# Attention and gated MLP on one core: the first phase rearranged, and the copies of turned chunks written in program order

## The chip, the core and the metric

The kernel runs on one core of a Trainium2 chip. The core has a matrix engine (TensorE: PE in the profile, with PEld for its weight loads), a vector engine (VectorE, DVE), a scalar engine (ScalarE, ACT), a general engine (GpSimd, POOL), a sequencer that issues most transfers (SyncE, SP) and 16 DMA engines. On-chip memory is SBUF (128 partitions); matrix products land in eight PSUM banks of 128 x 512 floats. The metric is device microseconds of one execution.

## What is computed

```python
xn = _layernorm(x)                       # x: 2048 rows, D = 576
s = _A_ref(xn, wqkv, wo)                 # attention, 32 heads of 18, then times wo
g = _silu(_B_ref(xn, W_gate, W_up, W_down))   # relu(gate) * up, F = 4608, then W_down
return x + s * g
```

Attention is a full softmax over 2048 keys for each head. All of it is in float32.

## The kernel before

A float32 product is made of three fast ones. Each operand is split into a high and a low part (`hi`, `lo`), and `hi*hi`, `hi*lo` and `lo*hi` are summed in one PSUM bank. A split is a copy into the fast type (ACT or POOL), then a subtraction (DVE or POOL, `split_full` and `split_pool`).

**First phase.** The 2048 rows come in four groups of 512, g = 0 to 3. For a group, DVE takes mean and variance of the rows and normalizes them (`stats`, `normalize`, lines 345 to 380), ACT copies the last 64 columns of each row block a second time (line 379), PE turns the normalized rows (`turn`, tile `tps`), and the turned chunks are split into tiles `x` (`keep_x`, 5 tiles a group). Then come jobs: four of queries and keys (`qk_block`, bank `pq`, weights `wqk0` to `wqk3`, and `wqk4` for each second group), and four of values (`v_job`, bank `pv`, weights `wv` in three parts). A job has 30 products of a first part and 24 of a second. The second part of a job runs after the first part of the next one (`pending`, `flush`). The statistics and transposes of group g+1 are dealt into the jobs of group g, one step after each 7 pairs of products (`deal`). Group 0 is done by `first_rows`. `spill` writes the turned chunks of a group to DRAM (`xTd`), since SBUF does not hold all four. The raw weights `rgw` have two buffers, and POOL splits them in the order of the code.

**Second phase.** 144 units follow, 36 for each group of rows: unit k is a group and a block of 128 of the 4608 hidden columns. `up(k)` makes 27 steps for each of two row halves: nine chunks c of 64 features by three products. They are interleaved with products for the maxima of the scores (`pm`) and for the scores (`psx`). An odd unit ends with the products of probabilities and values (`attend`, `po`), an even one with the second MLP product of two units (`down`, `py`).

**Copies.** `load_x(g, c)` copies chunk c of group g from `xTd` into a tile of the pool `xA`, as two DMAs of 64 partitions by 1024 floats (256 KB each, below: a half). `xA` has 11 tiles and a group needs nine, so two are free while a group is in use. In the last unit of a group the next group's chunks 0 and 1 are asked for at the start, and chunk c+2 after the products of chunk c (lines 677 to 691):

```python
        if last:
            for c in range(2):
                load_x(units[k + 1][0], c)
...
                if t and last and n % len(PRODUCTS) == 2 and c + 2 < KC:
                    load_x(units[k + 1][0], c + 2)
```

`load_up(k)` fetches the raw `gate` and `up` weights of unit k (tile `rg` with a single buffer, units 3 to 15 in tiles `p`), `split_up(k)` splits them on POOL into `gw` (two buffers), and `load_down` and `split_down` do so for W_down (`rd`, `dw`).

**Order.** Products, DVE and POOL instructions stand in the order of the code. SP's are issued through `sp`, which pins that order while `sp.kept` is true. From unit 10 on it is false, and a scheduler may place SP's transfers ahead of others wherever a tile is free, unless one is pinned by itself. An engine works through its queue in order: an instruction that waits holds up those behind it.

Of the kernel before, what the change touches and what calls it, by code (L numbers as in the profile page):

```python
# [9 lines left out]
F32 = mybir.dt.float32  # L10
# [9 lines left out]
def kernel(  # L20
# [108 lines left out]

    def split_pool(hi, lo, raw, behind=None):  # L130
        cast = gp.tensor_copy(hi, raw)
        if behind is not None:
            after(cast, behind)
        gp.tensor_tensor(lo, raw, hi.bitcast(F32), ALU.subtract)
# [164 lines left out]
    def load_x(g, c):  # L299
        xc = xtile(xA)  # L300
        for t in range(2):
            sp.dma_start(
                xc[t * R : (t + 1) * R].rearrange("p a s -> p (a s)").bitcast(F32),
                xTd[g, c // 2, c % 2 * R : c % 2 * R + R],
            )
        xcur.setdefault(g, []).append(xc)

    with ExitStack() as st:
# [4 lines left out]

        def weights(name, n, parts, pl=one, held=None, behind=None, **kw):

            sl = WS if len(parts[0]) == 2 else XC
            gw = homes_w[name] if name in homes_w else pl.tile([P, 2, WS, n], F32R, name=name, **kw)
            gw = gw[:, :, :sl]
            o = 0
            for cols in parts:  # L320
                m = sum(c[2] for c in cols[0])
                rg = one.tile([P, WS, P], F32, name="rgw", bufs=2)[:, :sl, :m]
                load_nat(rg, cols)
                hi, lo = gw[:, 0, :, o : o + m], gw[:, 1, :, o : o + m]

                if held is not None:
                    held += [
                        lambda: pinned(nc.scalar.activation(hi, rg, AF.Copy)),
                        lambda: vec(nc.vector.tensor_tensor(lo, rg, hi.bitcast(F32), ALU.subtract)),
                    ]  # L330
                else:
                    split_pool(hi, lo, rg, behind)
                o += m
            return gw
# [35 lines left out]
        def normalize(xn, xt, js, mv, rs):  # L370

            for i, j in enumerate(js):
                pinned(
                    nc.vector.tensor_scalar(
                        xn[:, j, :D], xt[:, j], mv[:, i, 0:1], rs[:, i : i + 1],
                        op0=ALU.subtract, op1=ALU.mult,
                    )
                )
                pinned(nc.scalar.activation(xn[:, j, D:], xn[:, j, C4:D], AF.Copy))
                yield  # L380

        def new_xn():
            return one.tile([P, 4, XC * P], F32, name="xn")

        def turn(ps, xn, j, c):
            tp(ps[:, j * P : (j + 1) * P], xn[:, j, c * P : (c + 1) * P], ident)

        def keep_x(g, ps):
            xc = xtile(xA if g % 2 else xB)
            split_full(xc[:, 0], xc[:, 1], ps)  # L390
            xs[g].append(xc)

        def first_rows(xt, split_hi, split_lo):

            xn = new_xn()
            banks = [shared("tps") for _ in range(XC)]
            halves = [(0, 1), (2, 3)]
            a, b = (stats(xt, js) for js in halves)

            def finish(st_):  # L400
                try:
                    while True:
                        next(st_)
                except StopIteration as s:
                    return s.value

            def norm(js, ln):
                for _ in normalize(xn, xt, js, *ln):
                    pass

            for _ in range(3):
                next(a)
            next(b)
            ln = finish(a)
            for _ in range(2):
                next(b)
            norm(halves[0], ln)
            split_hi()
            norm(halves[1], finish(b))
            done = split_lo()  # L420
            for j in range(4):
                for c in range(XC):
                    turn(banks[c], xn, j, c)
            for ps in banks:
                keep_x(0, ps)
            return done

        def rows_to_features(g, xt):

            js = range(4)  # L430
            ln = yield from stats(xt, js)
            yield
            xn = new_xn()
            yield from normalize(xn, xt, js, *ln)
            yield
            for c in range(0, XC, 2):
                for d in range(c, min(c + 2, XC)):
                    ps = bank("tps")
# [4 lines left out]

        def spill(g):
            for c in range(XC):
                m = P if c < XC - 1 else R
                sp.dma_start(xTd[g, c, :m], xs[g][c][:m].rearrange("p a s -> p (a s)").bitcast(F32))

        njob = [0]

        def next_pair(name):
            njob[0] += 1
            if njob[0] % 3:
                return [shared(name) for _ in range(2)]
            return [shared(name), psO.tile([P, 512], F32, tag="po", name=name)]
# [13 lines left out]
        def flush():  # L469
            if pending:  # L470
                gens, done = pending.pop()
                run(*gens, P2)
                done()

        def job(outs, ops, done):

# [4 lines left out]
            for ins in fence:  # L481
                after(seen, ins)
            fence.append(seen)
            flush()
            pending.append((gens, done))
# [77 lines left out]
        qk_weights(0, held=held)  # L563
        w0_done = first_rows(rows0, *held)
        qk_weights(1, behind=w0_done)
        nxt = load_rows(1)
        qk_weights(2)
        qk_weights(3)
        wv = one.tile([P, 2, WS, HC], F32R, name="wv")

        def v_weights(m):
            rg = one.tile([P, WS, P], F32, name="rgw", bufs=2)[:, :, :VH]
            load_nat(rg, [[(wqkv, 2 * D + o * HC + m * VH, VH)] for o in range(2)])
            fs = slice(m * VH, (m + 1) * VH)
            split_pool(wv[:, 0, :, fs], wv[:, 1, :, fs], rg)

        for g in range(NQ):
            last = g == NQ - 1
            fill = rows_to_features(g + 1, nxt) if not last else None
            deal[:] = [fill, 7, 0]  # L580
            if last:
# [3 lines left out]
            for b in range(4):  # L585
# [22 lines left out]
                if b == 2 and last:  # L608
                    load_k(0, NQ - 1)
                if b == 1 and g == 0:  # L610
                    v_weights(0)
                    v_weights(1)
                if b == 2 and g == 0:
                    v_weights(2)
# [6 lines left out]
            if last:  # L621
# [9 lines left out]
                for j in range(4):  # L631
                    v_job(wv, g, j, homes[j]())
                    if j == 0:
                        split_up(1)
                deal[0] = None
                flush()
                for c in range(KC + 2 - XC, KC):
                    load_x(0, c)
            else:
                for j in range(4):  # L640
# [3 lines left out]
                    if j == 1:  # L644
                        spill(g)
                    if j and g == NQ - 2:
# [22 lines left out]
    def up(k):  # L669

        g, f = units[k]
        gw = gus.pop(k)
        if k % 2 and k < N1:
            ps = [psO.tile([P, 512], F32, name="po"), shared("pg2")]
# [195 lines left out]
    def emit_unit(k, ex, ns, mx, nm):  # L870
# [7 lines left out]
        split_up(k + 1)  # L878
        load_up(k + 2)
        if k == 10:  # L880
# [22 lines left out]
        for i, (l, r) in enumerate(zip(*order)):  # L903
            next(l)
            next(r)
            if i == 8 or (i == 30 and k % 2 == 0):
                gate_step()
        up_end(k, ps)
        run_tasks(tasks)
# [176 lines left out]
```

## Time and profile before

| | |
|---|---|
| median of 3 runs | 2606.31 us (2605.06 to 2606.45) |
| the profiled execution | 2609.54 us |
| its span | 2607.8 us |
| mean granted clock of TensorE | 0.998 |
| PE busy | 2585.0 us, 99% |
| DVE busy | 1907.1 us, 73% |

The profile is of one execution, so working in microseconds is set against 2609.54, of which 1.7 lie around the span. The page's slices show DMA at 0.7 of its time in the first tenth and at 0.2 to 0.5 in most of the rest.

### The profile page before, as it was taken

Reading aid. Unit: us, or ns where it says so; the run is one execution under the profiler, and the core shown is the slowest. Engines: PE = TensorE matmul, PEld = TensorE weight load, DVE = VectorE, ACT = ScalarE, POOL = GpSimd, SP = SyncE. Lnnn points to the kernel's source line nnn. Section 1 sums busy time; section 2 is a strip of 40 time slices with the busy share of each in tenths; the row PEclk is TensorE's granted clock in tenths of the full one; section 3 lists DMA queues with packets and bytes.
Section 4 is the critical chain, followed back from the end, with each engine's and each line's share of the span. In section 5 each row is a group of like instructions: output and inputs, shape, how many; then the busy total and the mean of one; then the engine's idle time right before and its main releaser. Section 6 shows DMA issues by size and latency. Waiting matters only on the chain.

```text
span 2607.8 us, 54045 instructions
## 1 busy us (share of the span) xinstructions
PE 2585.0 (99%) x21788; PEld 2040.1 (78%) x21788; DVE 1907.1 (73%) x3145; ACT 1383.4 (53%) x2594; POOL 1205.6 (46%) x971
## 2 busy tenths in 40 slices
PE   7999999999999999999999999999999999999999
PEld 6898887777777877777777777877777777777788
DVE  5435677888878888888877888888877888888145
ACT  2321135666565665555666556665556655556552
POOL 4245764444464444444455444444445444444554
PEclk9999999999999999999999999999999999999999
DMA  7777512333452322232363232322353322222245
GB/s 254 250 226 155 126 47 66 75 73 73 101 127 69 79 62 68 66 75 68 80 150 85 67 71 71 76 67 64 74 119 100 71 74 68 71 58 58 71 139 189
DMA packets 263802, 253.08 MB, mean 97 GB/s; under 512 B 27648, under 2 KB 208896, under 8 KB 263552
## 3 DMA queue, kind: packets, MB, share of 16 engines
q1 hardware_dynamic: 255808, 222.48, 34.7%
q0 software_dynamic: 7744, 27.14, 3.1%
q8 instruction: 172, 2.82, 0.5%
q14 instruction: 78, 0.64, 0.1%
HBM read 203.01 MB, written 46.01 MB: 95 GB/s over the span
## 4 chain that ended last, share of the span: by engine, by line
PE 96%; DMA 2%; POOL 1%; DVE 1%; issue 0%; ACT 0%; SPq 0%; POOLq 0%; DVEq 0%; ACTq 0%
PE pg L68 32%; PE py L68 18%; PE po L68 18%; PE pm L68 11%; PE psx L68 9%; PE pq L68 4%; PE pv L68 2%; PE pw L68 2%; DMA x<-xTd 1%; DMA rg<-in_B_W_up_dram 0%; PE tps L76 0%; POOL wv L85 0%; DMA rgw<-in_A_wqkv_dram 0%; DMA gx<-gd 0%; POOL gw L85 0%
## 5 line engine op out<-in xcount | busy, mean ns | idle before, releaser
L272 DVE TENSOR_REDUCE mx<-pm 128x1 f32<-128x512 f32 x2048 | 1365.0, 690 | 364.2 <-PE pm L68 208.3
L68 PE MATMUL pg<-x,gw 64*128 64x512 f32 x7560 | 1375.0, 394 | 4.4 <-POOL gw L85 3.5
L97 ACT ACTIVATE p<-psx 128x512 f32<-128x512 f32 x2048 | 1098.0, 603 | 478.1 <-PE psx L68 431.7
L68 PEld LDWEIGHTS pg<-x,gw 64*128 64x128 f32 x7560 | 1033.5, 187 | 94.7 <-issue 4.7
L85 POOL TENSOR_TENSOR hh<-h,hh 128x512 fp32r<-128x512 f32 x144 | 185.5, 1288 | 1007.8 <-ACT hh L97 970.8
L68 PEld LDWEIGHTS py<-dw,hh 128*128 128x128 f32 x3456 | 459.5, 188 | 25.6 <-DVE mx L272 17.4
L68 PE MATMUL py<-dw,hh 128*128 128x288 f32 x3456 | 476.4, 297 | 0.0
L68 PE MATMUL po<-p,va 128*32 128x512 f32 x4096 | 452.7, 594 | 0.0
L85 POOL TENSOR_TENSOR gw<-rg,gw 128x1152 fp32r<-128x1152 f32 x131 | 350.0, 2671 | 10.5
L68 PEld LDWEIGHTS po<-p,va 128*32 128x32 f32 x4096 | 126.5, 110 | 291.4 <-issue 280.8
L730 DVE TENSOR_TENSOR y<-py,y 128x288 f32<-128x288 f32 x544 | 236.8, 453 | 111.9 <-PE py L68 111.8
L68 PE MATMUL psx<-qT,kq 56*128 56x512 f32 x608 | 230.5, 392 | 0.0
L68 PE MATMUL pm<-kq,qT 54*128 54x512 f32 x608 | 228.2, 398 | 0.4 <-DVE mx L272 0.4
L85 POOL TENSOR_TENSOR dw<-rd,dw 128x576 fp32r<-128x576 f32 x144 | 206.5, 1434 | 11.5
L97 ACT ACTIVATE hh<-h 128x512 fp32r<-128x512 f32 x144 | 90.9, 631 | 214.3 <-DVE h L701 214.3
L68 PE MATMUL psx<-kq,kA 56*128 56x512 f32 x512 | 195.6, 393 | 0.2 <-DVE h L701 0.2
L68 PE MATMUL pm<-kq 54*128 54x512 f32 x512 | 195.3, 402 | 0.0
L68 PE MATMUL psx<-kq 56*128 56x512 f32 x512 | 194.8, 392 | 0.0
L68 PE MATMUL pm<-kA,kq 54*128 54x512 f32 x512 | 193.8, 400 | 0.2 <-DVE mx L272 0.2
L85 POOL CAST dw<-rd 128x576 fp32r<-128x576 f32 x144 | 95.9, 666 | 165.9 <-PE py L68 157.1
L68 PE MATMUL pm<-kA,qT 54*128 54x512 f32 x416 | 159.6, 402 | 0.0
L68 PE MATMUL psx<-qT,kA 56*128 56x512 f32 x416 | 157.6, 393 | 0.6 <-DVE gx L967 0.6
(92 smaller groups left out, 2251.6 us busy)
## 6 DMA issues: line engine op xcount, KB each, us to landing
rd<-in_B_W_down_dram SPq DMA_DIRECT2D x144, 288.0 KB
rg<-in_B_W_gate_dram SPq DMA_DIRECT2D x131, 288.0 KB
rg<-in_B_W_up_dram SPq DMA_DIRECT2D x131, 288.0 KB
x<-xTd SPq DMA_DIRECT2D x72, 256.0 KB
qd<-hh POOLq DMA_DIRECT2D x16, 512.0 KB, 5.2
kd<-hh POOLq DMA_DIRECT2D x16, 512.0 KB, 6.1
xTd<-x SPq DMA_DIRECT2D x16, 512.0 KB
kq<-kd SPq DMA_DIRECT2D x210, 36.0 KB
```

Source lines behind the costliest of these rows:

```text
L68: return tc.keep_in_program_order(nc.tensor.matmul(*args, **kw))
L85: return lambda *args, **kw: tc.keep_in_program_order(op(*args, **kw))
L97: i = op(*args, **kw)
L272: vec(nc.vector.tensor_reduce(mx[:, h, b, j, c : c + 1], ps, axis=AX.X, op=ALU.max))
L730: vec(nc.vector.tensor_tensor(ys[j][:, cs], ps, ys[j][:, cs], ALU.add))
```

## The change

The change has eight parts.

1. `load_x` is pinned: its DMAs stand on SP where the code has them.
2. `first_rows` makes one chain of statistics for four row blocks where there were two chains of two. 57 transposes of the identity into a bank of their own stand ahead. The high part of `wqk0` stands on ACT after the square root, and its low part is cut into four, two on DVE and two on POOL. The transposes go row block by row block.
3. The first job's two banks come from the pool `psG`, which the turned chunks do not use there.
4. The three raw parts of `wv` are loaded into tiles of `xA` early, and `wqk3` is split by ACT and DVE. POOL splits `wv` earlier. Group 1's steps are dealt after each 9 pairs.
5. The copies of the last columns (`twice`) are made together, ahead of chunk 2's transposes. Group 3's five tiles are taken together, and its fifth chunk gets the first of them, the one that comes free first.
6. The spill of group 0 is held until the first part of its second value job is through.
7. Unit 2's raw weights are loaded during the last value jobs and split at the end of unit 0. They were loaded at the start of unit 0.
8. The first 16 units take other PSUM banks: even ones and unit 15 the pair that odd ones had.

```diff
...
     def load_x(g, c):
         xc = xtile(xA)
         for t in range(2):
-            sp.dma_start(
-                xc[t * R : (t + 1) * R].rearrange("p a s -> p (a s)").bitcast(F32),
-                xTd[g, c // 2, c % 2 * R : c % 2 * R + R],
+            pinned(
+                nc.sync.dma_start(
+                    xc[t * R : (t + 1) * R].rearrange("p a s -> p (a s)").bitcast(F32),
+                    xTd[g, c // 2, c % 2 * R : c % 2 * R + R],
+                )
             )
         xcur.setdefault(g, []).append(xc)
 
...
                 hi, lo = gw[:, 0, :, o : o + m], gw[:, 1, :, o : o + m]
 
                 if held is not None:
-                    held += [
-                        lambda: pinned(nc.scalar.activation(hi, rg, AF.Copy)),
-                        lambda: vec(nc.vector.tensor_tensor(lo, rg, hi.bitcast(F32), ALU.subtract)),
-                    ]
+                    held += [hi, lo, rg]
                 else:
-                    split_pool(hi, lo, rg, behind)
+                    split_pool(hi, lo, rg)
                 o += m
             return gw
 
...
                         op0=ALU.subtract, op1=ALU.mult,
                     )
                 )
-                pinned(nc.scalar.activation(xn[:, j, D:], xn[:, j, C4:D], AF.Copy))
                 yield
+
+        def twice(xn, j):
+            pinned(nc.scalar.activation(xn[:, j, D:], xn[:, j, C4:D], AF.Copy))
 
         def new_xn():
             return one.tile([P, 4, XC * P], F32, name="xn")
 
+        homes_x = []
+
         def turn(ps, xn, j, c):
             tp(ps[:, j * P : (j + 1) * P], xn[:, j, c * P : (c + 1) * P], ident)
 
         def keep_x(g, ps):
-            xc = xtile(xA if g % 2 else xB)
+            xc = homes_x.pop(0) if g == NQ - 1 else xtile(xA if g % 2 else xB)
             split_full(xc[:, 0], xc[:, 1], ps)
             xs[g].append(xc)
 
-        def first_rows(xt, split_hi, split_lo):
+        def first_rows(xt, hi, lo, rg):
 
             xn = new_xn()
             banks = [shared("tps") for _ in range(XC)]
-            halves = [(0, 1), (2, 3)]
-            a, b = (stats(xt, js) for js in halves)
-
-            def finish(st_):
+            js = range(4)
+            steps = stats(xt, js)
+            while True:
                 try:
-                    while True:
-                        next(st_)
+                    next(steps)
                 except StopIteration as s:
-                    return s.value
-
-            def norm(js, ln):
-                for _ in normalize(xn, xt, js, *ln):
-                    pass
-
-            for _ in range(3):
-                next(a)
-            next(b)
-            ln = finish(a)
-            for _ in range(2):
-                next(b)
-            norm(halves[0], ln)
-            split_hi()
-            norm(halves[1], finish(b))
-            done = split_lo()
-            for j in range(4):
+                    ln = s.value
+                    break
+            pinned(nc.scalar.activation(hi, rg, AF.Copy))
+            for j, _ in enumerate(normalize(xn, xt, js, *ln)):
+                twice(xn, j)
                 for c in range(XC):
                     turn(banks[c], xn, j, c)
+            rest = []
+            for s0 in (0, XC):
+                for on, ss in ((nc.vector, slice(s0, s0 + 2)), (None, slice(s0 + 2, min(s0 + XC, WS)))):
+                    args = lo[:, ss], rg[:, ss], hi[:, ss].bitcast(F32), ALU.subtract
+                    if on is None:
+                        rest.append(args)
+                    else:
+                        done = vec(on.tensor_tensor(*args))
+            for args in rest:
+                after(gp.tensor_tensor(*args), done)
             for ps in banks:
                 keep_x(0, ps)
-            return done
 
         def rows_to_features(g, xt):
 
             js = range(4)
             ln = yield from stats(xt, js)
             yield
+            if g == NQ - 1:
+                homes_x[:] = [xtile(xA) for _ in range(XC)]
+                homes_x.append(homes_x.pop(0))
             xn = new_xn()
             yield from normalize(xn, xt, js, *ln)
             yield
             for c in range(0, XC, 2):
+                if c == 2:
+                    for j in js:
+                        twice(xn, j)
                 for d in range(c, min(c + 2, XC)):
                     ps = bank("tps")
                     for j in js:
...
                     keep_x(g, ps)
                 yield
 
-        def spill(g):
+        def spill(g, behind=None):
             for c in range(XC):
                 m = P if c < XC - 1 else R
-                sp.dma_start(xTd[g, c, :m], xs[g][c][:m].rearrange("p a s -> p (a s)").bitcast(F32))
+                out_ = sp.dma_start(xTd[g, c, :m], xs[g][c][:m].rearrange("p a s -> p (a s)").bitcast(F32))
+                if behind is not None:
+                    after(out_, behind)
 
         njob = [0]
 
         def next_pair(name):
             njob[0] += 1
+            if njob[0] == 1:
+                return [bank(name) for _ in range(2)]
             if njob[0] % 3:
                 return [shared(name) for _ in range(2)]
             return [shared(name), psO.tile([P, 512], F32, tag="po", name=name)]
...
                 run(*gens, P2)
                 done()
 
+        marks = []
+
         def job(outs, ops, done):
 
             fence = []
...
             for ins in fence:
                 after(seen, ins)
             fence.append(seen)
+            marks.append(seen)
             flush()
             pending.append((gens, done))
 
...
 
         held = []
         qk_weights(0, held=held)
-        w0_done = first_rows(rows0, *held)
-        qk_weights(1, behind=w0_done)
+        warm = bank("warm")
+        for _ in range(57):
+            tp(warm[:, :P], ident, ident)
+        first_rows(rows0, *held)
+        qk_weights(1)
         nxt = load_rows(1)
+        wvs = []
+
+        def load_v(m):
+            rg = xtile(xA).bitcast(F32).rearrange("p a s -> p (a s)")[:, : WS * VH]
+            rg = rg.rearrange("p (c f) -> p c f", f=VH)
+            load_nat(rg, [[(wqkv, 2 * D + o * HC + m * VH, VH)] for o in range(2)])
+            wvs.append(rg)
+
+        load_v(0)
         qk_weights(2)
-        qk_weights(3)
+        held = []
+        qk_weights(3, held=held)
+        load_v(1)
+        load_v(2)
         wv = one.tile([P, 2, WS, HC], F32R, name="wv")
 
         def v_weights(m):
-            rg = one.tile([P, WS, P], F32, name="rgw", bufs=2)[:, :, :VH]
-            load_nat(rg, [[(wqkv, 2 * D + o * HC + m * VH, VH)] for o in range(2)])
             fs = slice(m * VH, (m + 1) * VH)
-            split_pool(wv[:, 0, :, fs], wv[:, 1, :, fs], rg)
+            split_pool(wv[:, 0, :, fs], wv[:, 1, :, fs], wvs[m])
 
         for g in range(NQ):
             last = g == NQ - 1
             fill = rows_to_features(g + 1, nxt) if not last else None
-            deal[:] = [fill, 7, 0]
+            deal[:] = [fill, 7 if g else 9, 0]
             if last:
                 spill(g)
             if g % 2:
...
                     load_up(1)
                 if b == 2 and last:
                     load_k(0, NQ - 1)
+                if b == 0 and g == 0:
+                    v_weights(0)
                 if b == 1 and g == 0:
-                    v_weights(0)
+                    hi, lo, rg = held
+                    pinned(nc.scalar.activation(hi, rg, AF.Copy))
+                    vec(nc.vector.tensor_tensor(lo, rg, hi.bitcast(F32), ALU.subtract))
                     v_weights(1)
-                if b == 2 and g == 0:
                     v_weights(2)
                 if b == 1 and g == 1:
                     nxt = load_rows(g + 2)
...
                     v_job(wv, g, j, homes[j]())
                     if j == 0:
                         split_up(1)
+                    if j == 2:
+                        load_up(2)
                 deal[0] = None
                 flush()
                 for c in range(KC + 2 - XC, KC):
...
                     if j == 0 and g == 0:
                         nxt = load_rows(g + 2)
                     if j == 1:
-                        spill(g)
+                        spill(g, marks[-1] if g == 0 else None)
                     if j and g == NQ - 2:
                         for c in range(2 * j - 2, 2 * j):
                             load_x(0, c)
...
 
         g, f = units[k]
         gw = gus.pop(k)
-        if k % 2 and k < N1:
+        if k < N1 and (k % 2 == 0 or k == N1 - 1):
             ps = [psO.tile([P, 512], F32, name="po"), shared("pg2")]
         else:
             ps = [bank("pg0"), bank("pg1")]
...
         if k not in rds and k not in dws:
             load_down(k)
         split_up(k + 1)
-        load_up(k + 2)
+        if k:
+            load_up(k + 2)
         if k == 10:
             sp.kept = False
         run_later()
...
             next(r)
             if i == 8 or (i == 30 and k % 2 == 0):
                 gate_step()
+        if k == 0:
+            split_up(2)
         up_end(k, ps)
         run_tasks(tasks)
         if k % 2:
```

On SP at the first group change (units 34 to 37), these rows stand before; `x<-xTd` is a half, `rg` the raw weights of a unit, `rd` those of W_down, and `qT<-nr` writes row maxima:

```order
L97 DMA rd<-in_B_W_down_dram 128x576
L97 DMA x<-xTd 64x1024
L97 DMA rg<-in_B_W_gate_dram 64x9x128
L97 DMA rg<-in_B_W_up_dram 64x9x128
L97 DMA x<-xTd 64x1024 x13
L97 DMA rd<-in_B_W_down_dram 128x576
L97 DMA rg<-in_B_W_gate_dram 64x9x128
L97 DMA rg<-in_B_W_up_dram 64x9x128
L97 DMA qT<-nr 2x8x32 x8
L97 DMA kq<-qd 18x1024 x3
L97 DMA kA<-kd 18x512 x6
L97 DMA kq<-qd 18x1024 x3
```

After the change the same place of SP reads:

```order
L97 DMA rd<-in_B_W_down_dram 128x576
L97 DMA rg<-in_B_W_gate_dram 64x9x128
L97 DMA rg<-in_B_W_up_dram 64x9x128
L301 DMA x<-xTd 64x1024 x18
L97 DMA rd<-in_B_W_down_dram 128x576
L97 DMA rg<-in_B_W_gate_dram 64x9x128
L97 DMA rg<-in_B_W_up_dram 64x9x128
L97 DMA qT<-nr 2x8x32 x8
L97 DMA kA<-kd 18x512 x6
L97 DMA kq<-qd 18x1024 x2
```

Before, one half stands ahead of the two `rg` transfers and 13 behind; the first four of the 18 stand far ahead, near unit 0 (below). After it all 18 stand in one row behind `rg`. The order moves alike at the other two group changes, where four of the 18 stood right behind the change before.

On POOL at the start, from the identity to the first two jobs' stores (`qd`, `kd`), before:

```order
masks.py:199 AFFINE_SELECT ident<-ident 128x128
L85 CAST wqk_209<-rgw 128x1152
L85 TENSOR_TENSOR wqk_209<-rgw,wqk_209 128x1152
L85 CAST wqk_219<-rgw 128x1152
L85 TENSOR_TENSOR wqk_219<-rgw,wqk_219 128x1152
L85 CAST wqk_109<-rgw 128x1152
L85 TENSOR_TENSOR wqk_109<-rgw,wqk_109 128x1152
L85 DMA qd<-hh 128x2x512
L85 DMA kd<-hh 128x2x512
L85 CAST wv<-rgw 128x9x96
L85 TENSOR_TENSOR wv<-rgw,wv 128x9x96
```

and after:

```order
masks.py:199 AFFINE_SELECT ident<-ident 128x128
L85 TENSOR_TENSOR wqk_110<-rgw,wqk_110 128x384
L85 TENSOR_TENSOR wqk_110<-rgw,wqk_110 128x256
L85 CAST wqk_255<-rgw 128x1152
L85 TENSOR_TENSOR wqk_255<-rgw,wqk_255 128x1152
L85 CAST wqk_270<-rgw 128x1152
L85 TENSOR_TENSOR wqk_270<-rgw,wqk_270 128x1152
L85 CAST wv<-x 128x9x96
L85 TENSOR_TENSOR wv<-x,wv 128x9x96
L85 DMA qd<-hh 128x2x512
L85 DMA kd<-hh 128x2x512
```

`wqk1` now stands behind two pieces of `wqk0`'s low part, `wqk3` is gone from POOL, and the first part of `wv` stands ahead of the first store.

On SP around units 0 to 2, before:

```order
L97 DMA kq<-kd 18x512 x6
L97 DMA qT<-qd 18x1024 x12
L97 DMA kA<-kd 18x512 x6
L97 DMA x<-xTd 64x1024 x8
L97 DMA rd<-in_B_W_down_dram 128x576
L97 DMA rg<-in_B_W_gate_dram 64x9x128
L97 DMA rg<-in_B_W_up_dram 64x9x128
L97 DMA x<-xTd 64x1024 x2
L97 DMA rd<-in_B_W_down_dram 128x576
L97 DMA p<-in_B_W_gate_dram 64x9x128
L97 DMA p<-in_B_W_up_dram 64x9x128
```

and after:

```order
L97 DMA kq<-kd 18x512 x6
L97 DMA qT<-qd 18x1024 x12
L97 DMA rg<-in_B_W_gate_dram 64x9x128
L97 DMA rg<-in_B_W_up_dram 64x9x128
L97 DMA kA<-kd 18x512 x6
L301 DMA x<-xTd 64x1024 x6
L97 DMA rd<-in_B_W_down_dram 128x576
L97 DMA rg<-in_B_W_gate_dram 64x9x128
L97 DMA rd<-in_B_W_down_dram 128x576
L97 DMA p<-in_B_W_gate_dram 64x9x128
L97 DMA p<-in_B_W_up_dram 64x9x128
```

Unit 2's `rg` has moved from behind eight halves to the place ahead of `kA` and of six halves; the four halves of the next group (two of the eight, and the two behind `rg`) have gone from here.

## Rows read from the trace of the kernel before

**Rows 1.** The page's part 1: busy time, share and instructions by engine.

```profile
PE 2585.0 (99%) x21788; PEld 2040.1 (78%) x21788; DVE 1907.1 (73%) x3145; ACT 1383.4 (53%) x2594; POOL 1205.6 (46%) x971
```

**Rows 2.** Timeline from the start: start, us, engine, line, operation [idle before <-releaser].

```profile
9.61 3.68 PE L76 MATMUL tps<-ident,xn 128*128 128x128 f32 x20 [9.61 <-DVE xn L374]
...
10.85 1.07 DVE L374 TENSOR_SCALAR xn<-xt,mv,ln 128x576 f32<-128x576 f32 x2
...
12.89 2.56 ACT L127 ACTIVATE x<-tps 128x512 fp32r<-128x512 f32 x5 [0.68 <-PE tps L76]
...
14.26 18.43 PE L68 MATMUL pq<-x,wqk 64*128 64x512 f32 x154 [0.97 <-DVE x L128]
...
14.49 2.68 POOL L85 TENSOR_TENSOR wqk<-rgw,wqk 128x1152 fp32r<-128x1152 f32 x1
```

**Rows 3.** Chain that ended last, first phase: start us, us, what.

```profile
35.36 4.86 DMA rgw<-in_A_wqkv_dram
...
43.33 3.37 PE pv L68 x26
...
156.25 24.95 PE pq L68 x214
```

**Rows 4.** Timeline of DVE, POOL and PE, 7 to 61 us.

```profile
7.44 0.17 DVE L366 TENSOR_SCALAR ln<-ln 128x2 f32<-128x2 f32 x1
...
23.58 2.54 DVE L366 TENSOR_SCALAR ln<-ln 128x4 f32<-128x4 f32 x1
...
31.57 2.15 POOL L85 TENSOR_TENSOR wv<-rgw,wv 128x864 fp32r<-128x864 f32 x1
...
32.63 1.09 PE L76 MATMUL tps<-ident,xn 128*128 128x128 f32 x8
...
49.30 10.94 PE L68 MATMUL pv<-wv,x 64*128 64x288 f32 x162
```

**Rows 5.** Stretches of PE alone: us, PE busy (x), PEclk, DMA share, GB/s.

```profile
9.60:12.30 2.70, 2.69 (x13) 1.00 1.00 351
...
10.00:20.00 10.00, 8.92 (x65) 1.00 0.64 194
...
40.00:50.00 10.00, 7.51 (x70) 0.83 0.88 277
```

**Rows 6.** Chain that ended last, units 0 to 4.

```profile
206.50 11.11 DMA rg<-in_B_W_up_dram
...
230.97 6.54 PE py L68 x48
...
251.74 6.57 PE py L68 x48
```

**Rows 7.** Timeline of PE, units 0 and 2.

```profile
202.91 1.63 PE L68 MATMUL pg<-x,gw 64*128 64x512 f32 x10 [0.47 <-ACT ev L532]
...
221.66 2.08 PE L68 MATMUL pg<-x,gw 64*128 64x512 f32 x8 [1.97 <-POOL gw L85]
```

**Rows 8.** Timeline of SP at the first group change.

```profile
695.29 0.48 SPq L97 DMA_DIRECT2D x<-xTd  x1
...
698.74 0.61 SPq L97 DMA_DIRECT2D rg<-in_B_W_gate_dram  x1
...
700.07 10.48 SPq L97 DMA_DIRECT2D x<-xTd  x13
```

**Rows 9.** Three group changes: us, PE, PEld, DVE, ACT, POOL busy, PEclk, DMA, GB/s.

```profile
703.00:718.00 15.00, 15.00 (x134) 8.51 (x133) 9.52 (x17) 8.56 (x16) 6.17 (x7) 1.00 1.04 231
...
1318.00:1332.00 14.00, 14.00 (x128) 8.12 (x122) 8.47 (x15) 7.60 (x15) 5.43 (x5) 1.00 1.04 235
...
1931.00:1945.00 14.00, 14.00 (x126) 7.77 (x124) 8.50 (x16) 7.66 (x15) 6.17 (x7) 1.00 1.04 242
```

**Rows 10.** Timeline of PE, last chunk at the first and second change.

```profile
719.95 0.74 PE L68 MATMUL pg<-x,gw 64*128 64x512 f32 x4 [0.40 <-DMA x<-xTd]
...
1333.55 0.86 PE L68 MATMUL pg<-x,gw 64*128 64x512 f32 x5
```

More of the change, by code (lines that the diff above doesn't have):

```diff
@@ L128, in split_full, with split_pool @@
         nc.vector.tensor_tensor(dlo, ps, dhi.bitcast(F32), ALU.subtract)
[L130 to L133, printed above, removed]
+    def split_pool(hi, lo, raw):
+        gp.tensor_copy(hi, raw)
         gp.tensor_tensor(lo, raw, hi.bitcast(F32), ALU.subtract)
@@ L312, with weights @@
         hx = pool(xBs, "hx", 4, "right")
-        def weights(name, n, parts, pl=one, held=None, behind=None, **kw):
+        def weights(name, n, parts, pl=one, held=None, **kw):
             sl = WS if len(parts[0]) == 2 else XC
```

## The prediction

> **What bounds the kernel now.** First the busy times: PE works 2585.0 of 2607.8 us [rows 1]. So only two kinds of time can be won: PE waiting, some 23 us in all, and PE at half clock. A loss is anything that makes PE wait anew. I read the chain that ended last for where something other than PE stands in it, then the timelines there. Four places come out.
>
> *The start.* The first transpose waits for the first normalized rows until 9.61 [rows 2]. Twenty of them take 3.68 us, where later eight take 1.09 [rows 4]: the first 13 take 2.69 [rows 5], 0.207 each against 0.136, which I read as half clock, though that row's clock column has 1.00. A backlog of them stands before the last rows' five. The last normalization ends at 11.92 (10.85 + 1.07), the first split begins at 12.89, and the first product at 14.26 [rows 2].
>
> *Group 0's value weights.* From 14.26 to 49.30 PE does 216 `pq` products at 0.1166 (24.95 / 214, [rows 3]), 20 transposes at 0.136 (1.09 / 8) and 30 `pv` products at 0.0675 (10.94 / 162, [rows 4]): 25.2 + 2.7 + 2.0 = 29.9 us. The stretch is 35.04, so 5.1 are lost. They lie at the `pv` products: the chain goes through the load of raw weights at 35.36 and resumes on PE at 43.33 [rows 3], and the ten microseconds from 40 hold 7.51 busy at a mean clock of 0.83 [rows 5].
>
> *Units 0 to 2.* Unit 2's weights are asked for at 206.50 and land 11.11 us later [rows 6], and PE waits for their split up to 221.66 [rows 7]. Two units and one `py` group take 251.74 - 230.97 = 20.77 us, 14.23 of it the two units [rows 6]. Three units should take 21.35; from 202.91 to 230.97 they took 28.06. So 6.7 are lost here, half clock included.
>
> *The group changes.* At the first, SP issues one half of the copies at 695.29, then the weights from 698.74, then 13 halves from 700.07 on [rows 8]. From 703 to 718 the DMA engines are busy all the time (1.04) and move 231 GB/s; at the other two changes it is 235 and 242 [rows 9]. A half is 262 144 bytes, so it takes 1.135, 1.116 and 1.083 us. PE is busy throughout, but only just: the last chunk's products wait for a copy at the first change, and at the second they start at 1333.55 with no wait noted [rows 10].
>
> **The change part by part.** *Start (parts 2, 3).* One chain of statistics in place of two saves seven small DVE steps at 0.17 [rows 4], 1.2; the wait for ACT's root, which the other chain's statistics covered, comes back, and I take 0.7 for it: 0.5 earlier. The 57 transposes begin with the identity, near 1.3, when PE has nothing else. If 13 of them run at 0.207 as the old ones did [rows 5] and 44 at 0.136, they end at 10.0, about when the first rows are normalized (some 9.9), so they cost nothing; all 57 at 0.207 would end at 13.1 and push the real ones back by 3.2. At full clock twenty take 2.7 instead of 3.68; of these 0.96, 0.65 are on the path, since ACT's tail copy stands between the last normalization and the first split. The first product comes 1.15 earlier, at 13.1. Own banks save the second bank's wait for one more split, an ACT step of 2.56 / 5 = 0.51 [rows 2]: 0.5, bounds 0 and 0.6. Against this, POOL begins `wqk1` only after two pieces of `wqk0`. By size, 384 and 256 of 1152 columns at 2.68 [rows 2] are 1.5 us, from about 12.0, when DVE's pieces end; copy and subtraction of `wqk1`, 3.8 with the 2.68, then end near 17.5 with the steps between. The second job, at 13.1 + 30 x 0.1166 = 16.6, asks for the low part in its third pair, near 17.0. The cost is 0.5 to 0.9, take 0.7; bounds 0 and 1.5. Start: 1.15 + 0.5 - 0.7 = **0.95 gained**.
>
> *Value weights (part 4).* With their own tiles the raw parts land without waiting for `rgw`, and POOL splits them earlier. A part's subtraction is 2.15 on POOL [rows 4], and its copy goes before it. I count 4.6 of the 5.1 as winnable, leaving 0.5 for bank waits. What takes it back: group 1's steps are dealt after 9 pairs, and their small DVE steps now meet a POOL queue without gaps. Row L366 takes 0.17 alone and 2.54 while POOL subtracts [rows 4], 2.4 more. One such hit before the transposes, 2.0 with what is slack, and 0.3 for banks: -2.3, with bounds 0 and -4.6. Rest: **2.3 gained**.
>
> *Spill, tail copies, tiles (parts 5, 6), banks (8).* The held spill goes out a few us later, and what it writes is read back only in the second phase; behind it SP has loads for later groups, covered by group 0's jobs. The tail copies stand on ACT, 53% busy [rows 1], and are wanted by the last chunk only. The fifth chunk's tile comes earlier. Taking other banks ends the wait of unit 0 for an evacuation: 0.47 [rows 7], **0.5 gained**; the even units' banks are evacuated under the products that follow.
>
> *Unit 2's weights (part 7).* They stand ahead of six halves and are split at the end of unit 0, ahead of `hh(0)` on POOL, which is delayed by a split (3.8), but is used only behind unit 2. The wait and the half clock go: **6.7 gained**. Next late would be chunk 8 of group 0, behind the weights by 576 KB; four halves have left this place, so I cost it at nothing (bound: one half, 1.1).
>
> *Copies (part 1).* All 18 halves stand on SP behind the weights that go out at 698.74, where five stood ahead [rows 8]. At a DMA that is full already, five more halves shift the last landing by 5 x 1.135 = 5.7, 5 x 1.116 = 5.6 and 5 x 1.083 = 5.4. I take 0.5 off the second, where no wait is noted [rows 10]: 5.7 + 5.1 + 5.4 = 16.2 lost. Nothing covers it: the products of the first unit read the chunks in order and have no other work beyond `pm` and `psx`. PE then works in pieces, and the clock may fall. From 40 to 50, with 7.51 us busy, it averaged 0.83, which cost 1.7 us; from 10 to 20, with 8.92 busy, it was 1.00 [rows 5]. A unit of some 10 us stretched to 15 lies below both, but its waits are of one half each, about 1.1, like the 0.97 ahead of the first product [rows 2] that cost no clock. I take 1.0 for the three changes, bounds 0 and 5.1 (three times 1.7). **17.2 lost.**
>
> The Trainium skill speaks of the rate: "DMA: Bandwidth & Descriptors", section Bandwidth, has 341 GB/s for one transfer of 1 MB. By it five halves would be an estimated 3.84 us and the sum some 5 us lower. The trace shows 231 to 242 at full engines, and the measurement decides.
>
> *Sum.* 0.95 + 2.3 + 0.5 + 6.7 = 10.45 gained, 17.2 lost: +6.75 on 2609.54, or 2616.3 in its profile's terms. On the median, 2606.31 + 6.75 = **2613.1 us**. Its own range, from the bounds: downwards 3.5 if the early gain is whole, 1.0 if the clock holds and 1.2 for one half of slack, 5.7; upwards 4.1 for the clock, 3.25 if start and values gain nothing, and 1.1 for chunk 8, 8.4: 2607.4 to 2621.5.
>
> **The rivals.** *A. The early gain is whole.* POOL and DVE do not collide, `wqk1` is in time, all 5.1 of the value weights come back: 1.65 + 5.1 + 0.5 + 6.7 = 13.95; the clock holds at the changes, 16.2 lost: +2.3, 2608.6. For it: DVE's slow step needs POOL at work in that very moment. Against: POOL's queue has no gap now.
>
> *B. The copies go faster.* The ten microseconds from 40 show 277 GB/s at a share of 0.88, 315 at a full one [rows 5]. At that rate five halves are 4.2 us: 12.5 + 1.0 lost, less 10.45: +3.0, 2609.3. Against it: the same 64-partition copies ran at 231 to 242 at all three changes [rows 9].
>
> *C. The copies are hidden anyway.* The halves start ahead of the weights after all, or the first unit of a group tolerates them: nothing lost, 2606.31 - 10.45 = 2595.9. Against it: the wait at 719.95 [rows 10] and SP's order.
>
> *D. The first phase gains nothing.* The steps of group 1, dealt later and held by POOL, come late to the values; PE waits for them and the clock falls, as from 40 to 50 [rows 5]. That takes all of the first two gains once DVE's chain loses over 3.3 us to POOL, less than two hits of 2.4 [rows 4]: 7.2 gained, 17.2 lost: +10.0, 2616.3. With the copies as in C this would still be faster; so the sign hangs on the copies.
>
> **How the numbers follow.** A change of 0.2%, 5.2 us, is about what a measurement can tell from none: faster is below 2601.1, slower above 2611.5. Forecast 0.50, A 0.17, B 0.10, C 0.11, D 0.12. C gives faster: 0.11. Slower are D and nearly all of the forecast's own range above 2611.5, with a little of A and B: 0.12 + 0.42 + 0.06 = 0.60. Same: 0.29. The range of 2604 to 2621.5 leaves out C and the ends where D meets a falling clock, together under 0.2.
>
> **What would show it.** On SP one row of 18 halves at each change, behind the weights. On PE, waits for `x<-xTd` that sum to about 5 us in the first unit of groups 1, 2 and 3, where now there is one of 0.40. No wait for `gw` in unit 2, none for `wv` at 41 to 43, the first transposes at full clock, and the first product near 13.1. If PE does not wait at the changes, or by less than 3 us each, step "copies" is wrong, and with it the sign. If unit 2 still waits, or group 0's values do, the gains are.

## The result and the profile after

The changed kernel takes 2619.73 us (median of 6 runs, 2616.8 to 2620.61), the kernel before 2606.34 beside it: a ratio of 1.005, 95% interval 1.0037 to 1.0063. It is 13.4 us slower, where 6.8 were forecast. Sign and place were right, both sizes were off: the group changes cost 1 to 3 us more than forecast, and the early gain was some 4 us less.

The page of the changed kernel, part 1:

```profile
PE 2595.6 (99%) x21845; PEld 2039.3 (78%) x21845; DVE 1907.2 (73%) x3141; ACT 1385.3 (53%) x2594; POOL 1204.6 (46%) x971
```

PE has 57 products more, the ones at the start, and they take 7.95 of the 10.6 us by which it is longer "busy" than in [rows 1]. Half-clock stretches count as work too, but both profiles have 10.2 us of them. The span is 2617.5 us.

**The group changes.** The timeline of SP at the first one, after:

```profile
685.96 0.36 SPq L97 DMA_DIRECT2D rd<-in_B_W_down_dram  x1
689.83 0.60 SPq L97 DMA_DIRECT2D rg<-in_B_W_gate_dram  x1
690.49 1.48 SPq L97 DMA_DIRECT2D rg<-in_B_W_up_dram  x1
692.02 14.99 SPq L301 DMA_DIRECT2D x<-xTd  x18
```

This is [rows 8] with all 18 halves behind the weights. SP stands still for 3.5 us ahead of the weights, and the 18 halves stand still with it. The raw weights `rg` have a single buffer, and POOL was still splitting what lay in it:

```profile
687.12 2.69 POOL L85 TENSOR_TENSOR gw<-rg,gw 128x1152 fp32r<-128x1152 f32 x1
```

The split ends at 689.81 and the weights go out at 689.83; it is the same to 0.03 us at the other two changes and in the kernel before. The timeline of PE in the first unit of groups 1, 2 and 3, its waits alone:

```profile
706.59 0.49 PE L68 MATMUL pg<-x,gw 64*128 64x512 f32 x1 [0.44 <-DMA x<-xTd]
708.62 0.50 PE L68 MATMUL pg<-x,gw 64*128 64x512 f32 x1 [0.59 <-DMA x<-xTd]
710.67 0.49 PE L68 MATMUL pg<-x,gw 64*128 64x512 f32 x1 [0.50 <-DMA x<-xTd]
713.57 0.50 PE L68 MATMUL pg<-x,gw 64*128 64x512 f32 x1 [1.68 <-DMA x<-xTd]
...
1334.16 0.50 PE L68 MATMUL pg<-x,gw 64*128 64x512 f32 x1 [0.83 <-DMA x<-xTd]
1336.42 0.96 PE L68 MATMUL pg<-x,gw 64*128 64x512 f32 x5 [0.82 <-DMA x<-xTd]
...
1953.57 0.79 PE L68 MATMUL pg<-x,gw 64*128 64x512 f32 x1 [1.54 <-DMA x<-xTd]
```

[Rows 10] had one wait of 0.40 at the first change and none at the second. The idle shown is only what lies between modelled ends of products; the whole is read from the starts. From its first product to the one after its last, the unit takes 16.58, 15.13 and 16.79 us at the three changes, and took 11.16, 10.28 and 10.57 in the first profile of the kernel before; after the first change the next products (`py`) take 1.58 more, at half clock. Together 18.1 us.

The windows of the changed kernel there (us, PE, PEld, DVE, ACT, POOL busy, PEclk, DMA share, GB/s):

```profile
692.00:707.00 15.00, 14.56 (x127) 7.91 (x126) 9.38 (x16) 7.88 (x15) 6.17 (x7) 1.00 1.01 252
707.00:722.00 15.00, 12.20 (x67) 8.85 (x64) 7.40 (x12) 6.01 (x10) 1.27 (x1) 0.77 0.74 170
1314.00:1329.00 15.00, 14.50 (x127) 7.83 (x125) 8.79 (x15) 7.66 (x15) 5.44 (x5) 1.00 1.06 252
...
1934.00:1949.00 15.00, 13.58 (x115) 6.61 (x109) 8.31 (x15) 7.10 (x13) 6.17 (x7) 1.00 1.05 244
1949.00:1964.00 15.00, 12.89 (x85) 10.61 (x81) 8.17 (x15) 4.82 (x8) 1.37 (x2) 0.89 0.73 150
```

The DMA engines are as full as in [rows 9] while the halves land. The clock falls behind the waits at the first and the third change: 0.77 and 0.89 of 15 us is 3.4 and 1.7 us worth of clock. At the second, with waits of 0.50 to 0.83, it does not fall.

**The start.** PE in the first phase, after:

```profile
12.85 0.50 PE L68 MATMUL pq<-x,wqk 64*128 64x512 f32 x2 [0.25 <-ACT x L127]
13.57 3.94 PE L68 MATMUL pq<-x,wqk 64*128 64x512 f32 x32 [0.22 <-DVE x L128]
18.01 18.30 PE L68 MATMUL pq<-x,wqk 64*128 64x512 f32 x158 [0.50 <-POOL wqk L85]
...
38.32 0.77 PE L76 MATMUL tps<-ident,xn 128*128 128x128 f32 x5 [0.30 <-DVE xn L371]
...
45.51 10.94 PE L68 MATMUL pv<-wv,x 64*128 64x288 f32 x162
```

The first product comes 1.4 us earlier than in [rows 2], the second job waits for `wqk1` at 18.01, and group 1's transposes wait for DVE. DVE's small steps there are slow while POOL splits `wv`, as one was in [rows 4]:

```profile
29.88 1.65 DVE L361 TENSOR_TENSOR ln<-ln 128x4 f32<-128x4 f32 x1
...
32.61 1.93 DVE L364 TENSOR_TENSOR ln<-ln,ln 128x4 f32<-128x4 f32 x1
```

**Units 0 to 2.** The waits of [rows 7] are gone, and one new wait stands in unit 0, for its last chunk (chunk 8):

```profile
207.07 0.50 PE L68 MATMUL pg<-x,gw 64*128 64x512 f32 x1 [1.49 <-DMA x<-xTd]
```

### The profile page after: what moved, and what is told of

The parts are those of the page before. It is cut to its first block, busy times and chain, and to the rows that moved or that the text cites. A ratio compares the mean times of both kernels' runs of the same rounds, so it can differ in the third digit from the quotient of the medians.

```text
span 2617.5 us, 54137 instructions
## 1 busy us (share of the span) xinstructions
PE 2595.6 (99%) x21845; PEld 2039.3 (78%) x21845; DVE 1907.2 (73%) x3141; ACT 1385.3 (53%) x2594; POOL 1204.6 (46%) x971
## 4 chain that ended last, share of the span: by engine, by line
PE 93%; DMA 3%; POOL 1%; DVE 1%; issue 1%; SPq 1%; ACT 0%; POOLq 0%; ACTq 0%; DVEq 0%
PE pg L68 31%; PE py L68 18%; PE po L68 17%; PE pm L68 11%; PE psx L68 9%; PE pq L68 3%; DMA x<-xTd 2%; PE pv L68 2%; PE pw L68 2%; POOL gw L85 0%; POOL dw L85 0%; SPq L301 0%; PE tps L76 0%; SPq L97 0%; DMA qd<-hh 0%
```

## The experiments

The theory: the place of the copies behind the weights costs the group changes 18 us, and unit 2's earlier weights give most of the early gain. The rivals: the pin itself costs, by holding up what follows it on SP; or the gain is the first phase's. All times are medians with the kernel before beside them, at 2606.0 to 2606.5.

### A second profile of the kernel before

> The kernel before once more, for a second look. Its first profiled execution took 2609.54 us against a median of 2606.34, 3.2 more, while the changed kernel's took 2619.22 against 2619.73. Theory: the extra 3.2 us is a half-clock stretch that only some executions have (in the first look one of 6.8 us behind the wait of unit 2 and one of 3.4 at group 0's values), so this look has one or none of them, or the same two and again about 2609.5. Rival: the profile itself slows this kernel everywhere; then the units far from the start are longer than in unprofiled runs and nothing single can be named.

2607.18 us. PE's waits for the value weights are not there, and those for unit 2's weights are:

```profile
43.02 2.15 PE L68 MATMUL pv<-wv,x 64*128 64x288 f32 x30
...
47.77 10.93 PE L68 MATMUL pv<-wv,x 64*128 64x288 f32 x162
...
217.86 1.22 PE L68 MATMUL pg<-x,gw 64*128 64x512 f32 x4 [2.08 <-POOL gw L85]
220.56 2.07 PE L68 MATMUL pg<-x,gw 64*128 64x512 f32 x8 [1.48 <-POOL gw L85]
```

The 30 `pv` products run in one piece. So the 5.1 us at group 0's values belonged to the one execution that was profiled, not to the kernel: the stretch from the first product to the long value products (15.44 to 47.77) is here 2.4 us over its 29.9 of work, and 1.1 to 1.2 in three further profiles with the same code there. The half clock behind unit 2 (6.8 us of it) is in both profiles. The theory of the expectation fits.

### The copies: pinned, not pinned, and elsewhere

`e1_unpin` is the changed kernel with the old way of issue, `e2_pin` the kernel before with the new one:

```diff
-            pinned(
-                nc.sync.dma_start(
+            sp.dma_start(
```

> The changed kernel with the copies of turned chunks issued as before, so that the scheduler places them: 5 of 18 halves ahead of the weights at each group change. Theory (the place of the copies costs 18.1 us at the three group changes, waits 14 and clock 4): those go, 2619.7 - 18.1 = 2601.6, and the first unit of each group is as long as in the kernel before. Rival 1 (the loss is elsewhere, in the first phase or the held spill): still about 2619. Rival 2 (pinning costs only the clock's share): 2615.

2600.45 us, ratio 0.9976 (0.9967 to 0.9985): 19.3 below the changed kernel. The one execution that was profiled took 8193 us, where the other eleven took 2598 to 2602, so there is a second run:

> The changed kernel with the copies placed by the scheduler, again: the profiled execution of the first time was a disturbed one. Theory: 2600.5, no wait over 1 us at the three group changes, the early gain of the changed kernel (some 7 us up to unit 3 against the second look at the kernel before) kept within 1 us.

2599.37 us, ratio 0.9976 (0.9966 to 0.9985). No wait of PE for the copies is left at the group changes. Everything that the changed kernel loses is the one edit of `load_x`.

> The kernel before with the copies pinned and nothing else changed. Theory: 14 to 18 us lost at the three group changes, at most 1.5 given back near unit 0 since four halves leave that place: 2606.3 + 16 = 2622, between 2619 and 2625. Rival (pinning alone is harmless and only collides with the other parts): 2606.

2619.82 us, ratio 1.0052 (1.0039 to 1.0064): 13.3 slower, at the foot of what was expected. Its first units of the groups lose 19.2 us, and some 4 come back near unit 0, where four halves are gone from around unit 2's weights, two ahead of them and two behind; units 0 to 2 take 23.49 us, in the second profile of the kernel before 27.74. Unit 2 still waits once for its weights, 1.87 us, but the clock does not fall there, where it stood at half level for 6.8 us in the kernel before: that is 3.4 of the 4. The expectation had 1.5 for this.

`e5_ask_early` keeps the pin and asks for chunks 0 and 1 earlier:

```diff
-        if last:
-            for c in range(2):
-                load_x(units[k + 1][0], c)
...
         split_up(k + 1)
+        if units[k][1] == NF - 3 and k + 3 < len(units):
+            for c in range(2):
+                load_x(units[k + 3][0], c)
```

> The changed kernel, copies pinned, but the next group's chunks 0 and 1 asked for two units earlier in the code, so that 4 halves stand ahead of the weights and 14 behind. Theory (what counts is how many halves stand behind the weights, not the pin): one half more than in the kernel before, 3 x 1.1 us over the unpinned version, so about 2605, with waits under 2 us in each first unit. Rival (a pinned row on SP holds up what follows it): no better than 2615.

2604.59 us, ratio 0.9992 (0.9984 to 1.0001). With 14 halves behind the weights the first units still lose 3.5 us, and the clock does not fall. `e8_weights_last` keeps the pin and the place of the copies, and moves the weights behind them:

```diff
+        late_up = units[k][1] == NF - 1 and k + 2 < len(units)
-        if k:
+        if k and not late_up:
             load_up(k + 2)
...
+        if late_up:
+            load_up(k + 2)
         up_end(k, ps)
```

> The changed kernel, copies pinned, but in the last unit of a group the weights of the unit after next are asked for behind its products, so that all 18 halves stand ahead of them. Theory (what costs is what stands ahead of the halves in SP's row): the 18 go out from the start of the last unit, land 6 us before they are needed, and the three group changes show no wait at all; 18 to 20 us below the changed kernel, about 2600, at or 1 below the unpinned version (2600.5). Rival 1 (the weights are late instead, and the unit that uses them waits): 2604 to 2610 with waits for `gw` two units into each group. Rival 2 (a row of 18 pinned transfers is itself the cost): still 2615 or more.

2599.22 us, ratio 0.9976 (0.9967 to 0.9984). SP at the first group change, and the window there:

```profile
686.46 16.82 SPq L301 DMA_DIRECT2D x<-xTd  x18
704.03 0.63 SPq L97 DMA_DIRECT2D rg<-in_B_W_gate_dram  x1
```

```profile
692.00:707.00 15.00, 15.00 (x134) 9.11 (x132) 9.65 (x17) 8.33 (x16) 1.28 (x2) 1.00 1.04 231
```

A row of 18 pinned transfers costs next to nothing if it stands ahead of the weights: PE is busy throughout this window, has one wait of 0.42 us for a copy at the three changes together, and waits for `gw` in no unit. The halves go out at 686.46 here, right behind `rd`, and at 692.02 in the changed kernel. Of these 5.6 us, 3.5 are the wait of SP for POOL's split, and the rest is the issue of the weights. The four profiles side by side, PE's waits from 600 to 2000 us (engine, line, waited for: us in total, times, longest), of the changed kernel, of `e2_pin`, of `e5_ask_early` and of `e8_weights_last`:

```profile
PE pg L68 <- DMA x<-xTd: 10.0, 13, 1.7
```

```profile
PE pg L68 <- DMA x<-xTd: 9.3, 13, 1.3
```

```profile
PE pg L68 <- DMA x<-xTd: 3.0, 4, 1.6
```

```profile
PE pg L68 <- DMA x<-xTd: 0.4, 1, 0.4
```

The wait goes with the number of halves behind the weights (18, 18, 14, none), with and without the rest of the change, and the pin has no price of its own. How much of it is the weights' own transfer and how much the wait for their buffer is not parted by these runs: by an estimate 589 824 bytes at 252 GB/s take 2.3 us, against the 3.5 of the wait.

### The early gain: whose is it?

`e4_only7` is the kernel before with part 7 alone, `e3_unpin_no7` the unpinned version without it:

```diff
+                    if j == 2:
+                        load_up(2)
...
+        if k:
             load_up(k + 2)
...
+        if k == 0:
+            split_up(2)
```

> The kernel before with the earlier load and split of unit 2's weights alone. Theory: 5 us faster than before, 2601.5, no wait for `gw` in unit 2. Rival (that step needs the other parts, since unit 0 then waits for its own last chunk behind the weights): 2 to 3 us faster at most, 2604, with a wait of over 1 us for `x<-xTd` in unit 0.

2599.56 us, ratio 0.9976 (0.9967 to 0.9985): 6.5 faster. Units 0 to 2 take 21.10 us, with no wait but the 0.45 for `ev`. The theory gave 5.

> The unpinned version without the earlier load and split of unit 2's weights. Theory (forecast's term for unit 2 is right, and the rest of the first phase gains little): 5 us slower than the unpinned version, 2605.5, with a wait for `gw` in unit 2 again. Rival (most of the early gain is the first phase's): 2 slower, 2602.5. A third way: the copies that the scheduler moves ahead near unit 0 fill that place anyway, and nothing changes, 2600.5.

2602.50 us, ratio 0.9987 (0.9978 to 0.9996). So the first phase's parts are worth 3.5 us where unit 2 waits for its weights, part 7 alone is worth 6.5, and both together 6.6 (6.0 in the first run): they do not add. Some of the 3.5 can be clock: in the profile, the fastest of the ten executions, unit 2 waits 0.99 and 1.97 us for `gw` and the clock does not fall. The other profiles show what stands in between. In the run with part 7 alone, the copies of group 0's last chunks go out at 195.79 and unit 0 begins at 199.87, 4.1 us later. In the changed kernel they go out at 195.75, unit 0 begins at 199.17, 3.4 later, and it waits 1.49 for chunk 8; in the unpinned version it is 194.31, 197.76 and a wait of 1.13. So part of what the start gains is waited for at chunk 8. That this is all of the missing 3.4 us is not shown.

The value weights are the other half. `b1_two_moves` is the kernel before with part 7 and the order of `e8_weights_last`; `b2_two_moves_warm` has the 57 transposes besides.

> The kernel before with two moves only: unit 2's weights earlier (as in the run with that step alone, 2599.6), and the copies pinned with all 18 halves ahead of the weights at each group change. Theory (these two are all that the changed kernel's parts are worth, the rearranged first phase adds nothing): 2598, 1 to 2 below the run with unit 2's weights alone, since the waits of 0.9 and 0.3 at the group changes go. Rival (the first phase's parts are worth their 3.5 us here too): 3 us above the version with all parts and the weights last, 2602.

2599.11 us, ratio 0.9974 (0.9963 to 0.9985). The two moves make all of the gain that any version had.

> The same, and the 57 transposes at the start. Theory (the clock is at its full level from the first transposes on, where without them it rose at 12.3 to 19.7): 1.0 to 1.7 below the version without them, 2596.5. Rival (the first phase waits for the value weights in any case, which were split at 41.5 in the run with unit 2's weights alone, just when PE asked): no difference over 0.5, 2598, with a wait for `wv` that is longer by what the start gained.

2600.78 us, ratio 0.9978 (0.9969 to 0.9987), not faster. PE, where the value jobs begin:

```profile
42.07 1.99 PE L68 MATMUL pv<-wv,x 64*128 64x288 f32 x26 [1.34 <-POOL wv L85]
```

PE came 1 us earlier and waited 1.34 for `wv`: the rival of the expectation. Two more, from the unpinned version, without the 57 transposes and with shared banks for the first job:

```diff
-        warm = bank("warm")
-        for _ in range(57):
-            tp(warm[:, :P], ident, ident)
```

> The unpinned version without the 57 transposes. Theory: the first transposes and some first products run at half clock again, the first product comes 1 us later, 2600.5 to 2601. Rival (the second job waits for its weights anyway, 0.5 us at 18): 2600.

2599.13 us, ratio 0.9971 (0.9960 to 0.9983): no difference. The first product came at 15.71 in its profile instead of 12.72, the long value stretch at 46.81 instead of 44.88, and unit 0's wait for chunk 8 fell from 1.13 to 0.38.

```diff
-            if njob[0] == 1:
-                return [bank(name) for _ in range(2)]
```

> The unpinned version with the first job's banks shared with the turned chunks again. Theory (forecast's 0.5): 2600.0. Rival (the second job's wait for its weights, 0.5 at 18, takes up what the bank gives): 2599.4, no difference.

2599.82 us, ratio 0.9975 (0.9965 to 0.9985). Theory and rival are 0.6 apart, which these intervals cannot part; the first product came at 13.62 without the banks, and no wait for `wqk1` followed it.

## Why the prediction was right, and where it was not

**Copies: right, and 1 to 3 us too small.** Forecast 17.2; changed kernel less unpinned version, 2619.73 - 2599.9 (the mean of its two medians), is 19.8, and the first units' lengths give 18.1. Most of the difference lies ahead of unit 0, which begins at 199.17 in the profile of the one and at 197.76 in that of the other; why is not shown. Two errors stand against each other, so that the term came out this near is partly luck. The waits were sized too long: chunk 8 came 4.4, 4.7 and 5.8 us later in its unit than before, of which 0.4 at the first and 1.2 at the third change is clock, so 13.3 us are waits where 16.2 were forecast. A half took 1.02 to 1.08 us, as windows of the changed kernel show 244 to 257 GB/s, where 231 to 242 had been taken from [rows 9]; and this holds for all 18, not only for the five more, so the last one landed 4.6, 4.9 and 5.4 us later behind the issue of the weights than before, where 5.7, 5.6 and 5.4 had been taken. The clock was sized too low: 1.0 was taken of a bound of 5.1, and the changed kernel lost 3.4 + 1.7 = 5.1 in its profile. The reason given, that single waits are as short as the 0.97 at the start, did not hold: the last wait of the unit was 1.68 and 1.54 us at the two changes where the clock fell, behind shorter ones of 0.4 to 0.7, with PE at work in between. The Trainium skill's 341 GB/s ("DMA: Bandwidth & Descriptors", section Bandwidth) is its figure for one transfer of 1 MB over 128 partitions. The trace does not show it for these copies of 64 partitions and 256 KB: full engines moved 231 to 257 GB/s in this place.

**Unit 2: right.** Forecast 6.7, measured 6.5 as a step by itself.

**Start, value weights, banks: wrong.** Forecast 3.75 us together; in the presence of part 7 they are worth nothing that was measured (2599.4 with them, 2599.6 without). The step that failed first is "value weights": it sized a gain from one profiled execution, whose 5.1 us the second profile did not have. In the run with part 7 alone the stretch from the first product to the long value products has 1.1 us over its work (15.14 to 46.10, against 29.9), so there was hardly anything to win. In the changed kernel it has 2.8 (12.85 to 45.51), among them the wait for `wqk1` (0.50, forecast 0.7) and the late steps of group 1, which the forecast had named as what takes gain back. The start came 1.4 to 2.6 us earlier than in the two profiles of the kernel before, more than the 1.15 that were forecast, and part of it was given back there and at chunk 8 of unit 0, the step that was costed at nothing with a bound of 1.1: 1.49 us in the changed kernel, 1.13 in the unpinned version.

**The sum.** 17.2 - 10.45 became 19.8 - 6.4. Rival D, in which the first phase gains nothing, is what happened on the one side, though the clock did not fall at the values as D had it, and the falling clock at the group changes on the other; the sum of both lies near the upper end of the range. A further 3.2 us of caution was to be had from the numbers shown: the profiled execution of the kernel before was that much over its median, and of the 2.4 us between its two profiles 1.7 lay ahead of unit 0, the stretch that the gain was sized from.

**A version that beats both.** The kernel before with two moves (unit 2's weights during the last value jobs; at a group change the copies ahead of the weights) takes 2599.1 us, 7 less than before and 20 less than the changed kernel. Part 7 alone does as well within the intervals.

## What to carry to other kernels

Where a queue's transfers keep the DMA engines full, what counts is what stands ahead of the urgent ones, its bytes and also what it waits for: 18 halves behind 576 KB of weights that themselves waited 3.5 us for their buffer cost 18 to 20 us in three places, and the same 18 ahead of them next to nothing. Before a stall is counted as a gain, look at a second execution, above all where the profiled one is slower than the median. And a time won ahead of a transfer can be lost again in the wait for that transfer.

## What was not expected of the hardware

The clock fell in the middle of units in which PE had been idle for 0.4 to 1.7 us at a time (1.00 to 0.50 at 714.5 and at 1953.5 us in the changed kernel), but not at the second change of the same kernel (waits of 0.50 to 0.83), and not with 14 halves behind the weights, where the waits of all three changes summed to 3.0 us with a longest of 1.6. With the pin alone (`e2_pin`) it fell at all three changes, and no wait there was longer than 1.3. The time at which the trace's record of the granted clock begins, at full level, is not fixed: 12.3 to 19.7 us in six profiles without the 57 transposes, 4.5 to 7.1 in seven with them, and the totals do not follow it. A stretch ahead of the record shows as 1.00, as [rows 5] from 9.60 to 12.30: that record begins at 12.3, so the row's 1.00 does not speak against the half clock that its 0.207 us a product suggest.
